# Windowed attention and a token expert layer: from eighty chunks in steps to forty units in a written order

## The chip, the cores and the metric

One core of a Trainium2 chip. The metric is device time in microseconds for one launch. The kernel before was run three times: 281.56, 281.57 and 285.97 us, median 281.57 us. The engines are named as the profile names them: PE (TensorE), with PEld for its weight loads, DVE (VectorE), ACT (ScalarE), POOL (GpSimd) and SP (SyncE, which issues most transfers).

## The reference

Eight batches, eight heads, 576 tokens, 64 numbers per head. Four heads see the 32 last keys, four see every fourth of the last 128 (again 32 keys). Then, for each batch, the 128 tokens with the highest gate score go through two dense layers:

```python
scores = scale * np.matmul(q, k.transpose(0, 1, 3, 2))
rel = pos[:, None] - pos[None, :]
mask_plain = (rel >= 0) & (rel < window)                                      # window 32
mask_dil = (rel >= 0) & (rel < window * dilation) & (rel % dilation == 0)     # dilation 4
scores = np.where(masks, scores, -1e9)
attn = softmax(scores)                       # maximum subtracted, sum + 1e-9
x = (attn @ v)                               # tokens x 512
...
scores = np.einsum('bsd,d->bs', x, w_gate)
for b in range(B):
    top_idx = np.argpartition(-scores[b], capacity)[:capacity]                # capacity 128
    xe = x[b, top_idx]
    ye = np.maximum(xe @ w1, 0.0) @ w2
    out[b, top_idx] = xe + g[:, None] * ye   # g = 1 / (1 + exp(-scores))
```

## The kernel before, in words

**Tiling.** A batch has ten chunks: four of the dilated heads with 128 queries each (one residue of the position modulo four), one with the last 16 queries of all residues, and five of the plain heads (four of 128 queries, one of 64). A group of 32 queries sees a window of 64 keys. `scores` (L165 to L194) lays a chunk's windows side by side in one PSUM bank of tag `s`, of which there are two; each product has 64 rows and 64 columns. Partitions are pairs of heads and queries.

**A chunk's way.** `maximum` (L219) adds the mask and takes the maximum of each window in one fused instruction of DVE, followed by a read of the accumulator. L224 subtracts the maxima, on POOL for nine chunks of ten once the first steps are past. `transposes` (L233 to L258) turns the differences on PE into a single bank `t` and ACT writes their exponentials. `attend` (L276, L281) multiplies by the values, each key with a column of ones so that the divisor comes along, into one of two banks `a`. `normalise` adds a small number to the divisor (L291), inverts it (L293) and divides, either on DVE in one instruction (L296) or on ACT in four (L301). SP stores the rows (L314).

**Choosing the tokens.** `route` sums each chunk's rows with the gate's weights on DVE (L356), brings the dilated scores into token order through DRAM (L367, L368), spreads all scores over the partitions with PE (L379), copies them to SBUF with ACT (L381), counts on DVE for each token how many are higher (L388), marks the 128 ranks (L396, mostly POOL), and finds and gathers the rows (L406 to L412). 

**The experts.** The weights are split into two float32r parts, a rounded one and the rest (L333, L335, L336), and each product is three matmuls (L473, L490, L503). Rows of batches 2 and 3, 4 and 5, 6 and 7 are worked on together, those of 0 and 1 alone. The results come from `tag="m"`, three banks.

**The order.** A loop over 84 and more steps issues the pieces of several chunks: in step g the scores of chunk g, the turning of chunk g - 2, the values of g - 3 and the division of g - 4. The dictionary `T` says in which steps loads, placings (copies of the queries into their places, L121) and the choice happen; `work` hands out the experts' pieces by a rate. In the first 20 steps `scores` also issues three products with no use of their own (L171) to keep PE busy. Every engine executes its instructions in the order in which this loop issues them.

Of the kernel before, what the change touches and what calls it, by code (L numbers as in the profile page):

```python
# [9 lines left out]
F32 = mybir.dt.float32  # L10
# [28 lines left out]
T = dict(  # L39
    spd=(0, 5),  # steps in which the vector engine subtracts the maxima  # L40
    lqx=(0, 0),  # delay of the first of the later loads of queries
    warm=9,  # products that bring the tensor engine to its full clock while the first loads run
    sp=(0, 1, 2, 3, 5, 6, 7, 8, 9),  # chunks whose maxima GpSimd subtracts
    mp=(0, 1, 2, 3, 4),  # token tiles that GpSimd marks
    ne=(0, 1, 2, 3, 4, 5, 7, 8, 9),  # chunks that the vector engine divides in the first nb steps
    nb=25,
    pl1=(7, 7, 8, 8),  # steps at which the next dilated queries are put into their places, by pair and half
    pl0=(13, 11, 13, 10),  # the same for the plain ones
    pe1=(1, 1, 1, 1),  # 1: the scalar engine does it, 0: the vector engine
    pe0=(1, 1, 1, 1),  # L50
    lq1=10,  # steps of the loads of queries
    lq0=14,
    nv=(0, 2, 3, 4, 7, 9),  # chunks that the vector engine divides; the scalar engine does the others
    rep=3,  # more products with the mask in the first rn steps, which bring the tensor engine to its full clock
    rn=20,
    ro=10,  # step of the dilated gate scores' way into the tokens' order
    g4=14,  # step of the leftover's gate scores
    b0=(14, 15, (15, 15, 15, 17, 16), (15, 16, 15, 17, 16), 18, 20),  # steps of the choice in the first batch: total, spread, ranks, marks, pick, first use
    last=(14, 16, (16, 16, 17, 16, 16), (17, 17, 17, 17, 17), 21, 24),  # the same in the last batch
    mid=(15, 16, (16, 17, 18, 19, 20), (17, 20, 18, 20, 20), 22, 26),  # and in the others  # L60
    raw=(12, 21, 5),  # first steps of the loads of the two weights, and the delay of their split
    rate=(0.9, 0.65, 0.95, 0.9, 1.0),  # pieces of the experts' work in half a step, by group
    single=(0, 1, 5, 7),  # batches after which a tile alone is worked on
    extra=0,  # pieces that come before the step's exponentials
    gd=5,  # delay of the gate scores
    gd0=5,
    iq=(3, 4),  # steps of the first loads of the second batch's queries
    ip=3,  # step at which the first plain queries are placed
)
# [3 lines left out]
def tile_window_attention_moe(ctx, tc, qt, kt, va, vb, w_gate, w1, w2, masks, mask_l, ident, slots, toks, outs, capacity):  # L73
# [5 lines left out]
    ps = ctx.enter_context(tc.tile_pool(name="ps", bufs=2, space=PSUM))  # L79
# [4 lines left out]
    id32 = cp.tile([P, P], F32, name="id32")  # L84
    id16 = cp.tile([P, P], BF16, name="id16")
    mk = cp.tile([P, 2 * GK], BF16, name="mk")
    mkl = cp.tile([P, 2 * LK], BF16, name="mkl")
    thr_sb = cp.tile([P, 2 * 512 + HB], F32, name="thr_sb")
# [3 lines left out]
    toks_sb = cp.tile([P, NTOK], F16, name="toks_sb")  # L92
    qs = [cp.tile([P, 2, S // G, 2, G], F32, name=f"qs{i}") for i in range(2)]
# [3 lines left out]
    dts = [[cp.tile([P, (G if i else 0) + 4 * GK], F32, name=f"dt{i}_{j}") for j in range(3)] for i in range(2)]  # L97
    mss = [[cp.tile([P, 4 * GK], F32, name=f"ms{i}_{j}") for j in range(3 - i)] for i in range(2)]
    pts = [[cp.tile([P, 4, P], F32, name=f"pt{i}_{j}") for j in range(2)] for i in range(2)]
# [4 lines left out]
    warm = cp.tile([P, 512], BF16, name="warm")  # L104
    raw = {}
# [3 lines left out]
    def clear(kind, eng):  # L109
        eng.memset(qs[kind][HB:P, :, :, 0, :], 0.0)  # L110
        eng.memset(qs[kind][0:HB, :, :, 1, :], 0.0)

    def load_q(b, kind, lo=0, hi=S):
        nc.sync.dma_start(out=qw[kind][:, :, lo:hi], in_=qt[b, kind].rearrange("d (p s) -> d p s", p=2)[:, :, lo:hi])

    def load_k(b, kind, lo=0, hi=S):
        nc.sync.dma_start(out=ks[kind][:, :, lo:hi], in_=kt[b, kind].rearrange("d (p s) -> d p s", p=2)[:, :, lo:hi])

    def place(kind, h, eng, p0=0, p1=2, lo=0, hi=S):
# [5 lines left out]
    nc.gpsimd.memset(thr_sb, TINY)  # L125
    nc.gpsimd.affine_select(out=thr_sb, in_=thr_sb, pattern=[[-1, 2 * 512 + HB]], compare_op=ALU.is_gt, fill=0.0,
                            base=512, channel_multiplier=1)
# [3 lines left out]
    for kind in (1, 0):  # L131
        for j in range(2):
            nc.gpsimd.memset(pts[kind][j], 0.0)
        for j in range(3 * kind):
            nc.gpsimd.memset(dts[kind][j][:, 0:G], NEG)
        if kind:
            clear(0, nc.gpsimd)
            for j in range(2):
                nc.gpsimd.memset(mss[1][j][:, GK + G:2 * GK], NEG)
        else:  # L140
            nc.gpsimd.memset(mss[0][2][:, 0:G], NEG)

    def load_v(b, kind):
# [52 lines left out]
    def maximum(b, c, st):  # L196
# [14 lines left out]
        for u in range(n):  # L211
# [3 lines left out]
            else:  # L215
                m = mk[:, 0 if kind else GK:][:, 0:GK]
                if windows(c)[u][0] == 0 and c <= 5:
                    lo, hi = (0, G) if kind else (G, GK)
# [524 lines left out]
```

## Time and profile before

| | |
|---|---|
| median of three runs | 281.57 us |
| profiled execution, first to last instruction | 280.1 us |
| busy PE, DVE, ACT, POOL | 251.1, 205.8, 154.8, 128.1 us |
| mean granted clock of PE, as a share of 2.4 GHz | 0.971 |
| moved by DMA | 53.75 MB, mean 192 GB/s |

The profiled execution's own time is known as its span, 280.1 us from the first to the last instruction; the median of the runs is 1.5 us longer. In rows of the trace, "busy" time counts an instruction from its start to its modelled end, so that overlapping instructions may each be longer than the distance between their starts. A row of a window gives, for each engine, busy time and number of instructions in that stretch.

### The profile page before, as it was taken

To read this page: it belongs to the slowest core of one execution; us is meant where nothing else is said; L and a number is where in the kernel's file an instruction comes from. 1 tells how busy PE (TensorE), PEld (TensorE's weight loads), DVE (VectorE), ACT (ScalarE), POOL (GpSimd) and SP (SyncE) were. 2 spreads that over 40 slices of the span, in tenths; PEclk is the share of its full clock that TensorE was granted. 3 is DMA by queue.
4 is the path that set the end of the run, shared out by engine and by line. 5 is a ranking of instruction groups with operands and counts; after the bars stand their busy time and mean duration, and the time that the engine had idled before them with its cause. 6 is when DMAs were issued, how large, how long until landed. Compare 5 with 4: busy or idle time off the path is not lost. (4 is left out here: it accounts for less than half of the span.)

```text
span 280.1 us, 9042 instructions
## 1 busy us (share of the span) xinstructions
PE 251.1 (90%) x3245; PEld 194.2 (69%) x3245; DVE 205.8 (73%) x1152; ACT 154.8 (55%) x437; POOL 128.1 (46%) x153
## 2 busy tenths in 40 slices
PE   7799984789996978799998899999999989989992
PEld 3577763566764756477776688886777879869981
DVE  3887989757999886977998898769657986815211
ACT  2558855636583585787777878657565454012100
POOL 8123338837489953572485346227643451021011
PEclk9999999759999899999999999999999999999998
DMA  6998399766769498449765973964463113020010
GB/s 186 372 380 230 94 293 362 254 218 194 271 184 326 130 323 307 136 117 363 254 207 133 408 239 101 320 255 136 125 220 144 63 46 95 0 77 37 0 40 37
DMA packets 29998, 53.75 MB, mean 192 GB/s; under 512 B 9089, under 2 KB 20097, under 8 KB 28929
## 3 DMA queue, kind: packets, MB, share of 16 engines
q1 hardware_dynamic: 28240, 48.85, 53.0%
q0 software_dynamic: 1280, 4.20, 4.6%
q8 instruction: 26, 0.43, 0.7%
q10 hardware_dynamic: 432, 0.12, 0.2%
q14 instruction: 20, 0.16, 0.2%
HBM read 41.60 MB, written 11.55 MB: 190 GB/s over the span
## 5 line engine op out<-in xcount | busy, mean ns | idle before, releaser
L224 POOL TENSOR_TENSOR dt<-ms,mx 128x256 f32<-128x256 f32 (+1 forms) x68 | 51.7, 760 | 95.0 <-DVE mx L219 71.4
L219 DVE CUSTOM_DVE_ANT_0 ms<-s,mk 128x64 f32<-128x64 f32 (+1 forms) x272 | 43.5, 215 | 13.0 <-PE s L191 8.9
L281 PE MATMUL a<-vs,pt 128*64 128x65 f32 x1088 | 50.7, 232 | 2.5 <-DVE x L296 1.3
L281 PEld LDWEIGHTS a<-vs,pt 128*64 128x64 f32 x1088 | 40.6, 141 | 17.2 <-issue 4.1
L191 PEld LDWEIGHTS s<-ks,qs 128*64 128x64 f32 x1088 | 39.1, 142 | 16.6 <-issue 10.1
L191 PE MATMUL s<-ks,qs 128*64 128x64 f32 (+1 forms) x1088 | 48.3, 231 | 2.4 <-DMA ks<-in_kt_dram 2.1
L258 ACT ACTIVATE pt<-t 64x128 f32<-64x128 f32 (+2 forms) x128 | 34.7, 271 | 24.7 <-PE t L253 21.3
L247 ACT ACTIVATE pt<-t 64x256 f32<-64x256 f32 (+1 forms) x80 | 28.5, 356 | 25.6 <-PE t L243 24.3
L121 ACT COPY qs<-qw 64x576 f32<-64x576 f32 (+3 forms) x59 | 38.6, 676 | 5.2 <-DMA qw<-in_qt_dram 4.5
L388 DVE SCALAR_TENSOR_TENSOR junk<-sb,sc,thr_sb 128x576 bf16<-128x576 f32 (+1 forms) x40 | 36.8, 920 | 5.5 <-ACT sb L381 5.1
L356 DVE CUSTOM_DVE_ANT_0 junk<-x,wg 128x256 bf16<-128x256 f32 (+1 forms) x72 | 40.6, 564 | 0.0
L396 POOL TENSOR_SCALAR oh<-slots_sb,rk 128x128 f16<-128x128 f32 (+1 forms) x35 | 28.1, 809 | 4.1 <-DVE junk L388 4.1
L490 PE MATMUL ph<-xh,w1h 128*128 128x256 f32 x96 | 29.1, 303 | 0.5 <-ACT xh L439 0.5
L503 PE MATMUL py<-w2h,hh 128*128 128x512 f32 x64 | 28.8, 449 | 0.0
L503 PE MATMUL py<-w2l,hh 128*128 128x512 f32 x64 | 25.8, 403 | 2.0 <-POOL w2l L336 2.0
L301 ACT ACTIVATE x<-a,rin 128x64 f32<-128x64 f32 x100 | 23.1, 314 | 7.9 <-DVE rin L293 5.0
L490 PE MATMUL ph<-xl,w1h 128*128 128x256 f32 x96 | 27.0, 281 | 0.2 <-DVE xl L440 0.2
L490 PE MATMUL ph<-xh,w1l 128*128 128x256 f32 x96 | 26.8, 279 | 0.0
L510 POOL DMA_INDIRECT out_dram<-y,ix x8 | 8.5, 1059 | 40.0 <-DVE y L508 26.4
L503 PE MATMUL py<-w2h,hl 128*128 128x512 f32 x64 | 25.4, 397 | 0.0
L219 DVE DVE_READ_ACCUMULATOR2_ANT mx<- 128x1 f32 x288 | 23.9, 83 | 0.3 <-issue 0.2
L296 DVE TENSOR_TENSOR x<-a,rin 128x256 f32<-128x256 f32 (+1 forms) x55 | 23.0, 418 | 0.3 <-DVE mx L219 0.2
(89 smaller groups left out, 407.1 us busy)
## 6 DMA issues: line engine op xcount, KB each, us to landing
vs<-in_va_dram SPq DMA_DIRECT2D x8, 1170.0 KB, 8.0
qw<-in_qt_dram SPq DMA_DIRECT2D x15, 576.0 KB, 7.0
ks<-in_kt_dram SPq DMA_DIRECT2D x15, 576.0 KB, 5.2
out_dram<-x SPq DMA_DIRECT2D x64, 128.0 KB, 4.6
vs<-in_va_dram SPq DMA_DIRECT2D x8, 520.0 KB, 5.4
raw<-in_w_dram SPq DMA_DIRECT2D x16, 256.0 KB, 3.3
vs<-in_vb_dram SPq DMA_DIRECT2D x8, 195.0 KB, 5.4
out_dram<-x SPq DMA_DIRECT2D x32, 16.0 KB, 3.2
```

The source lines that it names most:

```text
L121: eng(qs[kind][r, p0:p1, lo // G:hi // G, h, :], qw[kind][r, p0:p1, lo:hi].rearrange("d p (g q) -> d p g q", q=G))
L191: nc.tensor.matmul(st[GK * p:GK * (p + 1), u * GK + lo:u * GK + hi], q[:, p, qg].rearrange("d h q -> d (h q)"), k[:, p, k0 + lo:k0 + hi], ...
L219: nc.vector.tensor_tensor_reduce(out=ms[:, u * wk_ + lo:u * wk_ + hi], in0=s3[:, u, lo:hi], in1=m[:, lo:hi], scale=1.0, scalar=-3.0e38, op ...
L224: (nc.vector if T["spd"][0] <= b * NCH + c < T["spd"][1] or c not in T["sp"] else nc.gpsimd).tensor_tensor(out=out.rearrange("q (u k) -> q ...
L247: nc.scalar.activation(pt[r].rearrange("k a (i u q) -> k u i a q", i=2, u=2)[:, u, 0:n], tt[r, 0:n * P].rearrange("k (i a q) -> k i a q", ...
L258: nc.scalar.activation(pt[r, :, g * G:(g + 1) * G], tt[r, i * P:(i + 1) * P].rearrange("k (a q) -> k a q", a=4), AF.Exp, scale=SCALE)
L281: nc.tensor.matmul(av[r, head, :], pt[:, 2 * p + h, r], v[:, c if kind else 2 * (c - 5) + i, vc], start=True, stop=True)
L356: nc.vector.tensor_tensor_reduce(out=junk[:n], in0=xs.pop((b, c))[:n], in1=wg[:n, o:o + 256], scale=UP, scalar=0.0, op0=ALU.mult, op1=ALU. ...
L388: nc.vector.scalar_tensor_tensor(out=junk[:n], in0=st["sb"][:n], scalar=st["sc"][:n, t:t + 1], in1=thr_sb[:n, o:o + S], op0=ALU.subtract, ...
L396: (nc.vector if last or t not in T["mp"] else nc.gpsimd).tensor_scalar(out=st["oh", s][:n, t, :], in0=slots_sb[:n, s * P:(s + 1) * P], sca ...
L490: nc.tensor.matmul(out, w[:, i, f * P:(f + 1) * P], x[:, i, :], start=i == 0 and k == 0, stop=i == 3 and k == 2)
L503: nc.tensor.matmul(pys[j], x[:, i, j * P:(j + 1) * P], w[:, i, :], start=i == 0 and k == 0, stop=i == 7 and k == 2)
```

## The change

The work is cut into 40 units, five a batch: two of two dilated chunks each (`d`), one of all leftovers (`l`: the residues' last queries and the plain heads' last 64), two of two plain chunks each (`p`). Every function works on a whole unit:

- Scores: eight windows of 64 columns fill one bank `st`, which is the only one. It is cleared once, and windows that lack a half are covered by wide masks made at the start (`mkd`, `mkp`).
- Mask, maximum and difference: one addition of the mask (`M`), one `tensor_reduce` (`X`) and one subtraction (`U`, on POOL for 33 units, on DVE for 7) of 512 columns instead of an instruction per window.
- Exponentials (`E`): the same instructions cover both chunks, 256 or 512 columns each.
- Values (`V`) go into one pair of banks, of which there is one; the divisor (`D`) and the division (`N`) take both chunks at once, and the division is always on DVE. The leftover unit is stored by ten small transfers (`O`).
- Gate sums: 12 units multiply on POOL (`G`) and sum on DVE; 20 units use two fused sums on DVE as before. The leftover's sums are one for all 512 numbers, after a readback.
- Ranks (`R`) read the spread scores directly in PSUM (two banks); the copies on ACT go. The table for draws becomes bfloat16.
- The weights' rounding is on ACT for all sixteen pieces. Of the 40 marks eight are on DVE.
- The filler products of the first 20 steps go. The warm-up is 18 products of 256 columns instead of 9 of 512.
- Experts: batch 0 and batch 7 alone, 1 and 2, 3 and 4, 5 and 6 together. Their banks `m` are two instead of three.
- The loop and `T` go: every piece has a name, and a text of 1190 names says the order in which they are issued. It interleaves attention, choice and experts freely. A few places of it, ahead of the core of the diff:

```
S18 M18 R2.2 X18 U18g K2.0.1g K2.0.0g R2.4 K2.0.4g K2.0.2g V16 D16 q4.0.0 R2.3 N16 Y0.0.5 S19
T17 E17.3 E17.2 E17.0 E17.1 p4.1.0.1.0a M19 X19 U19g G15 Y0.0.6 Y0.0.7 T18 V17 D17 K2.0.3v O16.0
...
```

(`S19` scores of unit 19, `p` placing, `q`, `k`, `v` loads, `w` loads of weights, `h` and `l` their parts, `b`, `K`, `t` the choice, `F`, `r`, `s`, `z` the first layer, `Y` the second; a last letter names the engine.)

```diff
-LT = 2            # steps from a chunk's scores to their turning
...
+ORDER = """
...
-    ps = ctx.enter_context(tc.tile_pool(name="ps", bufs=2, space=PSUM))
+    ps = ctx.enter_context(tc.tile_pool(name="ps", bufs=1, space=PSUM))
...
+    st = ps.tile([P, 512], F32, tag="s", name="st")
...
+    def product(p, g, kind, c0, k0, n):
+        nc.tensor.matmul(st[GK * p:GK * (p + 1), c0:c0 + n], qs[kind][:, p, g].rearrange("d h q -> d (h q)"),
+                         ks[kind][:, p, k0:k0 + n], start=True, stop=True)
...
+    def mask(u):
+        what, b, d = kind_of(u)
+        ms = keep(f"ms_{u}", wk, [P, 512], F32, "ms", 2)
+        masks_ = [mkd] if what == "d" else [mkp[:, d:d + 8, :]] if what == "p" else [mkl, mkp[:, 1:3, :]]
+        for (s3, w0, n), m, (o3, _, _) in zip(parts(u, st), masks_, parts(u, ms)):
+            nc.vector.tensor_tensor(out=o3, in0=s3, in1=m, op=ALU.add)
+
+    def maximum(u):
+        mx = keep(f"mx_{u}", wk, [P, 8], F32, "mx", 3)
+        for o3, w0, n in parts(u, kept[f"ms_{u}"]):
+            nc.vector.tensor_reduce(out=mx[:, w0:w0 + n], in_=o3, axis=AX.X, op=ALU.max)
+
+    def subtract(u, eng):
...
+                eng.tensor_tensor(out=o3, in0=i3, in1=mx[:, w0:w0 + n].unsqueeze(2).to_broadcast(list(i3.shape)),
+                                  op=ALU.subtract)
...
+    def attend(u):
+        what, b, d = kind_of(u)
+        av = kept[f"a_{u}"] = keep(f"a_{u}", ps, [P, 2, 512], F32, "a", 1)[:, :, 0:VW].rearrange(
+            "q a (h d) -> q a h d", h=4)
...
+    def divide(u):
+        av, rin, na = kept[f"a_{u}"], kept[f"rin_{u}"], 1 if kind_of(u)[0] == "l" else 2
+        x = keep(f"x_{u}", wk, [P, 2, 4, D], F32, "x", 3)
+        nc.vector.tensor_tensor(out=x[:, 0:na], in0=av[:, 0:na, :, 0:D],
+                                in1=rin[:, 0:na].unsqueeze(3).to_broadcast([P, na, 4, D]), op=ALU.mult)
...
+    def gate_terms(u):
+        o = 256 if u % NU < 2 else 0
+        gm = keep(f"gm_{u}", wk, [P, 2, 256], F32, "gm", 1)
+        nc.gpsimd.tensor_tensor(out=gm, in0=kept[f"x_{u}"].rearrange("q a h d -> q a (h d)"),
+                                in1=wg[:, o:o + 256].unsqueeze(1).to_broadcast([P, 2, 256]), op=ALU.mult)
...
+    def gate_sums(u):
+        nc.vector.tensor_reduce(out=sums(u), in_=kept[f"gm_{u}"], axis=AX.X, op=ALU.add)
...
+    def spread(b):
+        pa = keep(f"pa_{b}", ps, [P, 1024], F32, "pa", 1)
+        for t in range(NTOK):
+            nc.tensor.transpose(pa[:, t * P:(t + 1) * P], scs[b % 2][:, t:t + 1].to_broadcast([P, P]), id32)
...
+        nc.vector.scalar_tensor_tensor(
+            out=junk[:n], in0=kept[f"pa_{b}"][:n, 0:S], scalar=scs[b % 2][:n, t:t + 1], in1=thr_sb[:n, o:o + S],
+            op0=ALU.subtract, op1=ALU.is_gt, accum_out=kept[f"rk_{b}"][:n, t:t + 1])
...
+    for name in (ORDER.split() if nt == 1 else default_order(nt, groups)):
+        pieces[name]()
```

## Rows read from the trace of the kernel before

**Rows 1.** The page, engine table: busy us, share of the span, instructions.

```profile
PE 251.1 (90%) x3245; PEld 194.2 (69%) x3245; DVE 205.8 (73%) x1152; ACT 154.8 (55%) x437; POOL 128.1 (46%) x153
```

**Rows 2.** Windows: busy us (instructions) by engine, PE clock, DMA share, GB/s.

```profile
0.00:7.90 7.90, 5.06 (x31) 2.24 (x31) 3.46 (x7) 2.62 (x4) 7.11 (x18) 1.00 0.69 211
7.90:222.50 214.60, 195.79 (x2848) 147.91 (x2848) 175.90 (x1063) 140.32 (x400) 109.64 (x125) 0.97 0.71 232
222.50:274.90 52.40, 50.24 (x369) 44.01 (x368) 25.73 (x86) 11.84 (x34) 10.37 (x11) 1.00 0.13 40
274.90:280.10 5.20, 0.00 (x0) 0.00 (x0) 0.72 (x1) 0.00 (x0) 0.97 (x1) 0.75 0.13 50
```

**Rows 3.** Timeline, PE and PEld: start us, us, engine, line, operation.

```profile
120.69 0.55 PEld L281 LDWEIGHTS a<-vs,pt 128*64 128x64 f32 x16 [0.36 <-ACT h L476]
...
121.77 0.20 PEld L253 LDWEIGHTS t<-id,dt 128*128 128x128 f32 x2
...
238.08 0.28 PE L490 MATMUL ph<-xh,w1h 128*128 128x256 f32 x1
...
238.20 0.28 PE L490 MATMUL ph<-xh,w1l 128*128 128x256 f32 x1
...
239.02 0.40 PE L503 MATMUL py<-w2l,hh 128*128 128x512 f32 x1
...
239.26 0.40 PE L503 MATMUL py<-w2h,hl 128*128 128x512 f32 x1
```

**Rows 4.** Groups by line and form, PE: busy us, mean ns, idle before.

```profile
L171 PE MATMUL s<-warm,id 128*128 128x256 bf16 x60 | 10.2, 279 | 0.0
```

**Rows 5.** Groups by line and form, DVE.

```profile
L356 DVE CUSTOM_DVE_ANT_0 junk<-x,wg 128x256 bf16<-128x256 f32 x64 | 37.4, 584 | 0.0
L388 DVE SCALAR_TENSOR_TENSOR junk<-sb,sc,thr_sb 128x576 bf16<-128x576 f32 x32 | 30.0, 938 | 5.4 <-ACT sb L381 5.1
...
L293 DVE RECIPROCAL rin<-den 128x4 f32<-128x4 f32 x64 | 11.4, 178 | 2.2
L291 DVE TENSOR_SCALAR den<-a 128x4 f32<-128x4 f32 x64 | 9.7, 151 | 3.0 <-PE a L281 2.0 <-PE s L177 0.6 <-PE t L253 0.4
...
L447 DVE CUSTOM_DVE_ANT_0 junk<-xe,wg 128x512 bf16<-128x512 f32 x8 | 6.8, 849 | 0.1
...
L440 DVE TENSOR_TENSOR xl<-px,xh 128x512 fp32r<-128x512 f32 x8 | 5.5, 692 | 10.2 <-ACT xh L439 10.0
```

**Rows 6.** Timeline, DVE and POOL, three places.

```profile
120.17 0.23 DVE L219 CUSTOM_DVE_ANT_0 ms<-s,mk 128x64 f32<-128x64 f32 x1
...
120.72 0.42 DVE L296 TENSOR_TENSOR x<-a,rin 128x256 f32<-128x256 f32 x1
...
16.65 0.61 POOL L224 TENSOR_TENSOR dt<-ms,mx 128x256 f32<-128x256 f32 x1 [8.66 <-DVE mx L219]
16.75 0.80 DVE L356 CUSTOM_DVE_ANT_0 junk<-x,wg 128x256 bf16<-128x256 f32 x1
...
126.75 0.41 DVE L356 CUSTOM_DVE_ANT_0 junk<-x,wg 128x256 bf16<-128x256 f32 x1
```

**Rows 7.** Groups by line and form, POOL and ACT.

```profile
L224 POOL TENSOR_TENSOR dt<-ms,mx 128x256 f32<-128x256 f32 x60 | 46.3, 771 | 92.5 <-DVE mx L219 69.2 <-DVE sc L372 13.7 <-PE s L191 5.2
...
L336 POOL TENSOR_TENSOR w1l<-raw,w1h 128x512 fp32r<-128x512 f32 x8 | 11.4, 1428 | 5.4 <-ACT w1h L335 3.2 <-DVE w1h L333 1.9 <-DVE ix L408 0.4
...
L301 ACT ACTIVATE x<-a,rin 128x64 f32<-128x64 f32 x100 | 23.1, 314 | 7.9 <-DVE rin L293 5.0 <-issue 2.6
```

**Rows 8.** Windows of 46 to 52 us, and PE's timeline there.

```profile
46.00:48.00 2.00, 0.22 (x3) 0.20 (x4) 1.97 (x11) 0.57 (x2) 1.72 (x2) 1.00 1.00 373
...
50.00:52.00 2.00, 2.00 (x30) 1.67 (x32) 0.71 (x5) 1.34 (x3) 1.82 (x2) 0.50 0.32 105
...
50.45 1.14 PE L281 MATMUL a<-vs,pt 128*64 128x65 f32 x16
51.37 1.03 PE L191 MATMUL s<-ks,qs 128*64 128x64 f32 x16
```

More of the change, by code (lines that the diff above doesn't have):

```diff
@@ L36 @@
 VW = 4 * (D + 1)
-LT = 2
[L39 to L69, printed above, removed]
+NU = 5
@@ new lines, in pick, with index, gather @@
+    def pick(b, s):
+        pi = keep(f"pi_{b}_{s}", ps, [P, 512], F32, "m", 2)
+        for t in range(NTOK):
+            nc.tensor.matmul(pi[:, 0:1], oh_sb[s][:, t, :], toks_sb[:, t:t + 1], start=t == 0, stop=t == NTOK - 1)
+    def index(b, s):
+        nc.vector.tensor_copy(keep(f"ix_{b}_{s}", wk, [P, 1], I32, "ix", 6), kept[f"pi_{b}_{s}"][:, 0:1])
+    def gather(b, s):
+        m = min(P, capacity - s * P)
+        xe = keep(f"xe_{b}_{s}", wk, [P, DM], F32, "xe", 4)
+        if m < P:
+            nc.vector.memset(xe, 0.0)
+        nc.gpsimd.indirect_dma_start(
+            out=xe[:m], out_offset=None, in_=outs[b][:, :],
+            in_offset=bass.IndirectOffsetOnAxis(ap=kept[f"ix_{b}_{s}"][:m, 0:1], axis=0))
@@ L543, in tile_window_attention_moe @@
-    for _ in range(T["warm"]):
-        nc.tensor.matmul(pw, warm[:, 0:P], warm, start=True, stop=True)
-    load_q(0, 1, P, S)
-    load_k(0, 1, SR, S)
-    nc.scalar.dma_start(out=mkl, in_=mask_l)
-    nc.vector.tensor_copy(id16, id32)
-    for h in range(2):
-        place(1, h, nc.scalar.copy if h else nc.vector.tensor_copy, lo=0, hi=P)
-    for h in range(2):
-        place(1, h, nc.scalar.copy if h else nc.vector.tensor_copy, lo=P)
-    load_v(0, 1)
-    load_q(0, 0)
-    load_k(0, 0)
-    if nt:
-        nc.sync.dma_start(out=wg, in_=w_gate)
@@ new lines, in outer, with result @@
+    def outer(e, j, i):
+        b, s = e[j]
+        if i == 0:
+            keep(f"py_{b}_{s}", ps, [P, 512], F32, "m", 2)
+        hh, hl = hidden(e)
+        for (x, w, k) in ((hh, w2h, 0), (hh, w2l, 1), (hl, w2h, 2)):
+            nc.tensor.matmul(kept[f"py_{b}_{s}"], x[:, i, j * P:(j + 1) * P], w[:, i, :],
+                             start=i == 0 and k == 0, stop=i == 7 and k == 2)
+    def result(b, s):
+        y = keep(f"y_{b}_{s}", wk, [P, DM], F32, "raw", 4)
+        nc.vector.scalar_tensor_tensor(out=y, in0=kept[f"py_{b}_{s}"], scalar=kept[f"g_{b}_{s}"][:, 3:4],
+                                       in1=kept[f"xe_{b}_{s}"], op0=ALU.mult, op1=ALU.add)
@@ new lines, in draws, with warm_up @@
+    def draws():
+        nc.gpsimd.memset(thr_sb, TINY)
+        nc.gpsimd.affine_select(out=thr_sb, in_=thr_sb, pattern=[[-1, 2 * 512 + HB]], compare_op=ALU.is_gt, fill=0.0,
+                                base=512, channel_multiplier=1)
+    def warm_up():
+        pw = ps.tile([P, 512], F32, tag="m", bufs=2, name="pw")
+        for _ in range(WARM):
+            nc.tensor.matmul(pw[:, 0:256], warm[:, 0:P], warm, start=True, stop=True)
+    copies = {"a": nc.scalar.copy, "v": nc.vector.tensor_copy, "g": nc.gpsimd.tensor_copy}
@@ new lines, in tile_window_attention_moe @@
+    for u in range(B * NU):
+        what = kind_of(u)[0]
+        for name, f in (("S", scores), ("M", mask), ("X", maximum), ("T", turn_scores), ("V", attend), ("D", divisors),
+                        ("N", divide)):
+            piece(f"{name}{u}", f, u)
+        for a, eng in engines.items():
+            piece(f"U{u}{a}", subtract, u, eng)
+        for i in range(2 if what == "p" else 4):
+            piece(f"E{u}.{i}", weights, u, i)
+        for i in range(10 if what == "l" else 1):
+            piece(f"O{u}.{i}", store, u, i)
+        if what != "l" and nt:
+            piece(f"G{u}", gate_terms, u)
+            piece(f"H{u}g", gate_sums, u)
+            piece(f"H{u}v", gate_alone, u)
@@ new lines, in tile_window_attention_moe @@
+    for i in range(16 if nt else 0):
+        piece(f"w{i}", load_weights, i)
+        for a, eng in copies.items():
+            piece(f"h{i}{a}", weight_high, i, eng)
+        for a, eng in engines.items():
+            piece(f"l{i}{a}", weight_low, i, eng)
+    groups, ready = [], []
+    for b in range(B if nt else 0):
+        for n, f in enumerate((readback, gate_last, put_out, put_back, total, spread)):
+            piece(f"b{b}.{n}", f, b)
+        for t in range(NTOK):
+            piece(f"R{b}.{t}", rank, b, t)
+        for s in range(nt):
+            for t in range(NTOK):
+                for a, eng in engines.items():
+                    piece(f"K{b}.{s}.{t}{a}", mark, b, s, t, eng)
+            for n, f in enumerate((pick, index, gather, turn_rows, result, scatter)):
+                piece(f"t{b}.{s}.{n}", f, b, s)
+            for i in range(3):
+                piece(f"g{b}.{s}.{i}", gate_row, b, s, i)
+            ready.append((b, s))
+        while ready and (len(ready) > 1 or b in SINGLE):
+            groups.append(ready[:2])
+            del ready[:2]
```

914 lines of the change are left out of this document (462 added, 452 removed).

## The prediction

> **What bounds the kernel now.** I read the page's engine table first: no engine is busy throughout, PE at 90% and DVE at 73% lead [rows 1]. "Busy" counts overlapping pipelines, so next I took the windows, cut at three events: the first mask on the vector engine (7.9 us), the last block of scores (222.5 us) and the last matmul (274.9 us) [rows 2]. They show three regimes. Up to 7.9 us the first loads run. From 7.9 to 222.5 us all attention is issued, and DVE is busy 175.9 of 214.6 us, 82%. From 222.5 to 274.9 us PE is almost never idle: this is mostly expert work that attention pushed behind itself. The last 5.2 us hold only the final result and its scatter.
>
> For PE's real load I read the timeline, since spacing, not duration, is what a pipelined matmul costs [rows 3]. Sixteen instructions of scores or of values take 0.55 us (the span of their weight loads), a transposition about 0.10 us, a product of the experts 0.23 us with 512 columns (two starts 0.24 apart) and 0.115 with 256 (0.12 apart). Every float32 product is two instructions. Over the program: 136 blocks of sixteen 75; the half-size last units 7; 152 turns 15; experts 192 and 48 wide products 55, 288 narrow ones 33; gathered rows, spreads and picks 12; 60 filler products 7; warm-up 4. Together about 208 us. Some 50 of it lie behind 222.5 and 5 ahead of 7.9, so the middle stretch holds about 153 us of PE work in 214.6 us: PE waits there for 62 us. DVE waits for 39. So the stretch is set by two engines waiting for each other, the fuller of which is DVE. PE's total alone would permit far less than 280.
>
> **What the change does, part by part.**
>
> *Masks and maxima.* Before, one fused instruction per window; four windows take 0.55 us (120.17 to 120.72) [rows 6], 1.10 for the two chunks of a new unit. After: one add of 512 columns from PSUM, like the 692 ns subtraction [rows 5], and one maximum over 512 columns. No row shows such a maximum. Bounds: 0.42, the 256-column row [rows 6], and 0.85, the fused 512-column sum [rows 5]; I take 0.69, the nearest in size. So 1.38 against 1.10 in 32 units, and about 1.0 against 1.05 (0.55 by spacing for the leftover, half a chunk, a difference) in 8: DVE **+9 us** (0 to +14).
>
> *Divisors.* 151 and 178 ns now serve two chunks [rows 5]: 40 pairs instead of 80, **-13**. *Division.* DVE takes all: 32 of 0.69 and 8 of 0.42 is 25.4 against 55 of 0.42, **+2**; ACT loses 100 pieces, 23 us [rows 7].
>
> *Gate sums.* Before 80 sums, mean 0.58 for a chunk [rows 5]. After, 12 units send the product to POOL and leave DVE one 512-column sum (0.69); 20 units keep two sums of 0.58; the leftover's eight grow to 0.85. 38 against 45: **-7**. *Ranks* read PSUM instead of a copy; before 0.94 and not less than 0.69 x 576/512 = 0.78. At 0.85, 40 of them are **-3** (-6 to 0), and 6 us of copies leave ACT. *Weight roundings* move to ACT: eight of about 0.69, **-5.5**. Seven differences and eight marks come to DVE instead of a few: **+2**. DVE's sum: 205.8 - 15.5 = about 190.
>
> Why sums vary: the same 256-column gate sum took 0.41 us alone and 0.80 beside a POOL difference that started 0.10 earlier [rows 6]. The Trainium skill ("SBUF — State Buffer", section "Who interferes with whom") says that a vector instruction with two SBUF inputs contends with a GpSimd instruction that reads SBUF, and one with a single SBUF input does not. Ranks, masks and divisions would then be free of it, and by it the ranks would come at the lower bound, 0.78, 3 us less in all; the trace agrees for the gate sums.
>
> *POOL.* 33 differences and 12 gate products of 512 columns. Bounds: 0.77, a 256-column one, and 1.43, the weight remainder of 512 [rows 7]; I take 1.43, which has the size. 64 us, marks 27 (32 of about 0.86, estimated from half-size differences), remainders 25, indirect transfers 17, placings and memsets 20: about 153, from 128. In units 4 to 17 the written order gives it 13 differences, 4 products, all 16 remainders, 9 marks, 3 placings, 2 transfers: 62 us, beside 59 on DVE. So POOL nearly ties there, and hides only if little goes wrong.
>
> *PE.* The same products; the 60 fillers go (10.2 us busy [rows 4], 7 by spacing). About 201. *DMA* moves the same data; its share of 0.71 in the stretch [rows 2] becomes 0.71 x 214.6/187 = 0.81. The ten small stores of a leftover unit stand in SP's queue, between loads; a load behind a store that waits comes late, a cost I put at zero since loads are issued a unit or more ahead, and at a unit (4.5 us) each if not.
>
> *Buffers.* Scores have one PSUM bank instead of two, the values' result one pair instead of two, the experts' bank two instead of three. So the next scores wait for the mask that reads the last ones, and the next values for the division: 0.69 and latency, and 0.33 + 0.69 and latency. In the order other PE pieces stand between. I walked units 18 to 22 with the prices above: five scores start at 0, 2.9, 7.8, 10.8 and 14.2 us, and PE is idle about 1.0 us in 14.2.
>
> *The end.* The last group holds one batch instead of two, and less waits for the last tokens. Behind the last scores the order leaves PE 32 pieces of three 512-column products (22.1), 96 narrow and 24 wide products (16.5), two blocks of values, and turns, picks and spreads (6): 45 us. Its own turn of hidden rows must wait for a copy, a subtraction and semaphores, about 3 us.
>
> **The sum.** DVE before the first mask stays near 4.5 and behind the last scores near 26 (before: 25.7 + 0.7 [rows 2]), so the stretch keeps 190 - 30.5 = 160 us. Its length is 160/u. Before, u was 0.82. The walked units give above 0.9, the start with POOL level and loads near their limit less; I take 0.86: 186 us, in which PE's 151 us are 81% (before 71%). End: 7.9 + 186 + 45 + 3 + 5.2 = 247 of span; with unrounded terms 248.3. The profiled execution spans 280.1 against a median of 281.57, 1.5 more, which I keep: **250 us** (u from 0.80 to 0.92: 264 to 238).
>
> **The rivals.**
>
> *The clock falls.* PE stood 46 to 48 us nearly idle (0.22 busy) at a granted clock of 1.00; at 50 to 52 it had 0.50, that is 1.2 instead of 2.4 GHz, and two blocks of sixteen started 0.92 apart instead of about 0.55 [rows 8]. The fillers held such gaps shut in the first 20 chunks. Without them PE has some 32 us of work in units 0 to 13, beside 41 on DVE. At the low level that is 32 x 0.92/0.55 = 54 us; with 0.95 us of waits a unit (38 in 40 units, below) and 5 us ahead it is 72, against 7.9 + 41/0.86 = 56: about 16 us more, **266 us**. For it: thin PE work early. Against it: in the windows as a whole the clock stayed at 0.97 [rows 2]. The Trainium skill ("TensorE: Matmul & The Clock Gate", section "A second HAM failure mode: psum-queue depth-cycling") tells of a kernel whose short idles between groups made the clock go back and forth; it speaks against this change. By that rule the time is this rival's.
>
> *The waits only move.* Larger pieces and single buffers keep PE waiting as long as before, 62 us or somewhat more. Then 5 + 151 + 62 = 218 for the last scores, and 218 + 53.2 + 1.5 = 273; up to 14 us more waiting is no change, **280**. For it: DVE's load falls by only 15 us, POOL's grows by 25. Against it: the walked units.
>
> *Turns (slower).* PE and DVE take turns at the single buffers. Place: scores behind the mask, values behind the division. Price for a unit: 0.69 + 0.25 and 0.33 + 0.69 + 0.30, 2.26 us, 90 over 40 units. If all of it shows, the last scores come at 5 + 151 + 90 = 246 and the time is **301 us**. It decides from the point where 287.2 is passed: 287.2 - 1.5 - 53.2 - 156 = 76.5 of the 90 exposed. For it: one bank each. Against: my forecast exposes 38, and the order has other pieces there.
>
> **How the numbers follow.** Chances: forecast 0.60 with its range 238 to 264; tighter, 234 to 238, 0.05; clock 0.11; waits move, 275 to 287, 0.12; turns beyond 287, 0.12. A range of 234 to 279 leaves out turns and most of the waits, 0.2. A change within 2% (276 to 287 us) can't be told from none. Faster 0.76, same 0.12, slower 0.12.
>
> **What would show it.** Right: windows with DVE near 86% until the last scores at about 194 us; masks and maxima near 0.69 each; POOL near 150 us busy; 45 us of dense PE behind the last scores. Wrong: a clock of 0.50 over several early windows; scores waiting for the vector engine's mask by a microsecond or more in most units; maxima over 0.85; POOL 512-column pieces over 1.75; or vector instructions waiting for POOL's products.

## The result, and the profile after

| | before | after |
|---|---|---|
| median | 282.71 us (4 runs, three of them those above) | 262.82 us (4 runs, 259.4 to 267.14) |
| ratio, 95% interval | | 0.9224 (0.916 to 0.9288) |
| profiled execution, span | 281.57, 280.1 us | 264.4, 262.7 us |
| forecast | | 250 us, own range 238 to 264, wide range 234 to 279 |

The ratio leaves out executions that the chip disturbed (of the four of the changed kernel it keeps 261.25 and 259.4 us), so it stands below the quotient of the medians, 0.930. The gain is 20 us by the medians and 22 by the ratio. The change is faster, as forecast, and the time lies in the range, but near its upper end: by the median it is 13 us longer than the number, by the ratio 10. Those 10 to 13 us are what the runs below look for. Where kernels are compared, the difference of their ratios, times 282 us, stands beside that of their medians.

The page of the changed kernel: busy time of each engine; the granted clock of PE and the busy share of the DMA engines in 40 slices; the chain that ended last.

```profile
PE 223.5 (85%) x3194; PEld 191.8 (73%) x3194; DVE 193.0 (73%) x520; ACT 105.7 (40%) x228; POOL 125.6 (48%) x154
...
PEclk9999986689999999799999999999999999999999
DMA  6997899888977799989644899886593154111001
...
PE 41%; DMA 30%; DVE 11%; issue 7%; SPq 5%; POOL 3%; ACT 2%; POOLq 0%; DVEq 0%; ACTq 0%
```

DVE has 193.0 us of work against 205.8 [rows 1], in 520 instructions instead of 1152. DMA has 30% of the chain. The page of the kernel before follows its chain for only 18% of the span and gives no comparison; a variant of it with other groups of experts, run below, has 9%.

The windows of after, cut at the same three events as before (columns as in [rows 2]):

```profile
0.00:8.47 8.47, 6.00 (x50) 4.37 (x50) 4.18 (x12) 2.12 (x3) 3.78 (x10) 1.00 0.73 228
8.47:208.80 200.33, 170.25 (x2793) 147.38 (x2795) 163.92 (x438) 95.75 (x210) 109.86 (x131) 0.96 0.80 244
208.80:257.40 48.60, 47.27 (x358) 40.02 (x353) 24.14 (x71) 7.86 (x16) 11.03 (x13) 1.00 0.21 66
257.40:262.70 5.30, 0.01 (x1) 0.00 (x0) 0.75 (x1) 0.00 (x0) 0.97 (x1) 0.98 0.13 49
```

The cut at 208.80 is the start of the last block of scores, as before; the runs below are cut at the start of that block's last product, 0.9 us later. Against [rows 2] the middle stretch fell from 214.6 to 200.3 us and what lies behind it from 57.6 to 53.9. In the stretch DVE is busy 163.92 of 200.33 us, 0.82: the same utilisation as before, where I had forecast 0.86. That is the open question: DVE has less to do, but waits as large a share of the time.

Pieces of the chain that ended last, in order of time (start, us, what), say on what:

```profile
30.21 6.23 DMA vs<-in_va_dram
36.57 1.50 PE a L399 x32
40.13 8.91 DMA ks<-in_kt_dram
49.17 1.98 PE st L269 x32
...
93.82 11.00 DMA ks<-in_kt_dram
104.95 1.57 PE st L269 x29
...
118.76 9.08 DMA ks<-in_kt_dram
127.97 1.15 PE st L269 x28
```

Four times this chain runs through a load of keys or values, 6 to 11 us from issue to landing. The scores of unit 9 start at 33.4 us, those of unit 10 at 49.2, behind the load issued at 40.13 (an expectation below calls them units 7 and 8; by the written order they are 9 and 10). PE was not idle all that time, since values and turns stand between. What ended its idle time (us in total, times, longest):

```profile
PE a L399 <- DVE x L412: 5.4, 5, 2.4
PE st L269 <- DMA ks<-in_kt_dram: 3.7, 5, 1.3
PE a L384 <- DMA vs<-in_vb_dram: 2.9, 2, 1.7
...
PE st L269 <- DVE ms L309: 2.4, 3, 0.9
...
PE a L399 <- DMA vs<-in_va_dram: 2.0, 1, 2.0
```

Loads ended 8.9 us of PE's idle time, with a smaller row of 0.3. If they cost more than that, it is by way of the other engines and buffers.

### The profile page after: what moved, and what is told of

It reads as the page before. It is cut to its first block, busy times and chain, and to the rows that moved or that the text cites. A ratio compares the mean times of both kernels' runs of the same rounds, so it can differ in the third digit from the quotient of the medians.

```text
span 262.7 us, 7956 instructions
## 1 busy us (share of the span) xinstructions
PE 223.5 (85%) x3194; PEld 191.8 (73%) x3194; DVE 193.0 (73%) x520; ACT 105.7 (40%) x228; POOL 125.6 (48%) x154
## 2 busy tenths in 40 slices
DMA packets 31284, 54.22 MB, mean 206 GB/s; under 512 B 9360, under 2 KB 20880, under 8 KB 30224
## 4 chain that ended last, share of the span: by engine, by line
PE 41%; DMA 30%; DVE 11%; issue 7%; SPq 5%; POOL 3%; ACT 2%; POOLq 0%; DVEq 0%; ACTq 0%
DMA ks<-in_kt_dram 13%; PE py L638 11%; PE ph L585 8%; PE a L399 7%; PE st L269 6%; DMA out_dram<-x 6%; DMA vs<-in_va_dram 5%; DMA xd<-out_dram 4%; DVE x L412 2%; DMA raw<-in_w_dram 2%; POOL w2l L453 2%; ACT ptd L368 2%; PE t L339 1%; SPq L429 1%; DVE ms L309 1%
## 5 line engine op out<-in xcount | busy, mean ns | idle before, releaser
L269 PE MATMUL st<-ks,qs 128*64 128x64 f32 (+1 forms) x1088 | 43.6, 234 | 6.7 <-DMA ks<-in_kt_dram 3.7
L269 PEld LDWEIGHTS st<-ks,qs 128*64 128x64 f32 x1088 | 38.9, 148 | 11.4 <-issue 4.9
L242 ACT COPY qs<-qw 64x576 f32<-64x576 f32 (+1 forms) x46 | 29.6, 655 | 20.2 <-DMA qw<-in_qt_dram 9.8
L368 ACT ACTIVATE ptd<-t 64x256 f32<-64x256 f32 (+2 forms) x64 | 23.6, 377 | 31.6 <-PE t L339 22.9
L399 PE MATMUL a<-vs,ptd 128*64 128x65 f32 x512 | 21.6, 238 | 11.9 <-DVE x L412 5.0
L516 DVE SCALAR_TENSOR_TENSOR junk<-pa,sc,thr_sb 128x576 bf16<-128x576 f32 (+1 forms) x40 | 30.8, 804 | 0.1
L328 POOL TENSOR_TENSOR dt<-ms,mx 128x512 f32<-128x512 f32 (+2 forms) x30 | 21.4, 727 | 19.2 <-DVE mx L314 13.7
L412 DVE TENSOR_TENSOR x<-a,rin 128x512 f32<-128x512 f32 (+1 forms) x40 | 25.4, 636 | 5.4 <-DMA out_dram<-x 2.4
L314 DVE TENSOR_REDUCE mx<-ms 128x8 f32<-128x512 f32 (+2 forms) x48 | 26.1, 558 | 0.7
L399 PE MATMUL a<-vs,ptp 128*64 128x65 f32 x512 | 20.0, 235 | 1.9 <-ACT ptp L368 0.8
```

Of the source, the lines that this page charges most:

```text
L242: eng(qs[kind][r, p0:p1, lo // G:hi // G, h, :], qw[kind][r, p0:p1, lo:hi].rearrange("d p (g q) -> d p g q", q=G))
L269: nc.tensor.matmul(st[GK * p:GK * (p + 1), c0:c0 + n], qs[kind][:, p, g].rearrange("d h q -> d (h q)"), ks[kind][:, p, k0:k0 + n], start=T ...
L314: nc.vector.tensor_reduce(out=mx[:, w0:w0 + n], in_=o3, axis=AX.X, op=ALU.max)
L328: eng.tensor_tensor(out=o3, in0=i3, in1=mx[:, w0:w0 + n].unsqueeze(2).to_broadcast(list(i3.shape)), op=ALU.subtract)
L368: nc.scalar.activation(out, src, AF.Exp, scale=SCALE)
L399: nc.tensor.matmul(av[i * HB:(i + 1) * HB, a, 2 * h + p], pt, values(1 if what == "d" else 0, j, 2 * h + p), start=True, stop=True)
```

## The experiments

The leading theory: loads of keys, values and queries, which I had priced at zero, land late and hold PE, and through it DVE. The rivals: the clock falls without the fillers; the chain through the single PSUM banks sets the pace; DVE's work does. Two more questions are why loads come late (bytes, or place in SP's queue), and where the 20 us that were gained come from.

### The changed kernel again

> The changed kernel again, unchanged, as the anchor of this set and for a second profile: 258 to 263 us (ratio to the kernel before 0.915 to 0.93). Every theory gives the same here; what it decides is where the granted clock falls. If the clock is at 1.00 all through this profile and the time is still about 260, the fall to 0.6 around 40 to 59 us in the first profile belonged to that execution and not to the kernel.

263.05 us median (257.68 to 266.32), ratio 0.9192 (0.9066 to 0.9319). Its profile has the clock low at other places than the first:

```profile
PEclk9999986988959977999999999979999999999998
```

The first had its dips in slices 6 to 9 and 17; this one is low in several places between slices 6 and 16, and once in slice 27. Around slices 6 to 10 the clock is low in both; where else it falls differs from one execution to the next.

### Without the later loads

```diff
-    v0.1.1 ... k1.1.0 ... q1.0.0 ... k1.0.0 ... v1.1.0 ...
+    (all q, k, v loads of batches 1 to 7 struck out of the written order)
```

> All loads of queries, keys and values behind batch 0's are left out, and their copies into the block layout work on batch 0's data again (the output is that of batch 0's inputs). Theory 1 (late loads are what keeps VectorE at 0.82 of the stretch): 160 to 164 us of work at 0.88 to 0.9 gives a stretch of 180 to 186, so 238 to 247 us. Rival 3 (the chain scores, mask, turn, weights, values over single PSUM buffers sets the pace): 256 to 261 us, for no load stands in that chain. Between these: both have a share, by where it falls.

245.53 us median (243.43 to 247.01), ratio 0.868 (0.8593 to 0.8766). The stretch, in its windows:

```profile
6.86:192.00 185.14, 166.59 (x2825) 144.83 (x2825) 166.12 (x442) 96.29 (x211) 109.03 (x134) 0.96 0.35 105
```

Same PE, DVE, ACT and POOL work, and 185.1 us instead of 200.3: utilisation 0.90. Loads are worth 15 us by the ratios (0.9224 - 0.868) and 17 by the medians. The clock of the stretch is 0.96 in both, so the difference is not the clock's. Rival 3 is left with little: the chain over single banks allows 185 us.

### The same loads, thin

```diff
     def load_k(b, kind, lo, hi):
+        hi = hi if b == 0 else lo + G
         nc.sync.dma_start(out=ks[kind][:, :, lo:hi], ...)
     # load_q alike; load_v: one tile instead of four or nine where b > 0
```

> Every load of queries, keys and values behind batch 0's keeps its place, its waits and its semaphores, but carries only a first slice (32 of 576 columns, one value tile of four or nine); the rest of each buffer keeps batch 0's data, so the output is not the reference's. The run without these loads stood at 245.5 us. If it is the bytes (each load takes long to land, and the DMA engines are near their limit): 244 to 249 us, as without the loads. If it is the place in SyncE's queue and the single buffers (a load is issued late): 255 to 261 us, as with full loads.

247.18 us median (245.62 to 247.64), ratio 0.882 (0.8748 to 0.8891): 15.6 us less than the changed kernel by the medians, 11 by the ratios, which is most of what leaving the loads out gave. Place in the queue, buffers, waits and number of issues are those of the changed kernel; only bytes are gone (28.37 MB moved instead of 54.22).

```profile
7.56:190.80 183.24, 165.74 (x2824) 143.85 (x2825) 164.11 (x442) 95.97 (x210) 109.30 (x133) 0.97 0.45 128
```

The same DVE work as after, 164.1 us, now takes 183.2 us, utilisation 0.896. So these 11 to 16 us are a matter of bytes on the way. DMA issues (columns: what, count, KB each, median us to landing), first of after, then of this run:

```profile
vs<-in_va_dram SPq DMA_DIRECT2D x8, 1170.0 KB, 9.2
qw<-in_qt_dram SPq DMA_DIRECT2D x15, 576.0 KB, 5.8
ks<-in_kt_dram SPq DMA_DIRECT2D x15, 576.0 KB, 7.0
out_dram<-x SPq DMA_DIRECT2D x32, 256.0 KB, 5.1
...
raw<-in_w_dram SPq DMA_DIRECT2D x16, 256.0 KB, 6.4
```

```profile
out_dram<-x SPq DMA_DIRECT2D x32, 256.0 KB, 2.3
raw<-in_w_dram SPq DMA_DIRECT2D x16, 256.0 KB, 4.3
...
ks<-in_kt_dram SPq DMA_DIRECT2D x14, 32.0 KB, 3.5
```

Stores and weight loads were not touched, yet land in 2.3 instead of 5.1 us and 4.3 instead of 6.4. Thin loads thus shorten every transfer beside them. How much of the time comes from the loads' own landing and how much from the others' (the stores free the result's buffers, the read-backs feed the ranks) this run does not separate. PE's idle time that a load ended falls only from 8.9 to 3.3 us, which points to a large part of the others.

### Thin loads in the kernel before

The same edit in the kernel before.

> The kernel before, with the same thin loads behind batch 0's (32 of 576 columns, one value tile; the output is not the reference's). If the loads' bytes were as dear to the kernel before as to the changed one (15 us): 264 to 269 us, and the gain of the change is not from them. If the kernel before was held by its engines and the loads were hidden: 278 to 284, and the loads became a bound only by the change.

277.34 us median (276.26 to 277.45), ratio 0.9865 (0.9787 to 0.9943).

```profile
7.38:218.80 211.42, 195.85 (x2852) 147.62 (x2854) 176.48 (x1063) 140.40 (x399) 110.35 (x126) 0.97 0.39 113
```

The bytes cost the kernel before 3.7 us (1.6 to 6 by the interval of its ratio), and the changed one 11 to 16. Neither expected band is met (it lies just under the second), but the second theory is the nearer: the kernel before mostly hid its loads, and the change uncovered them. Transfers were slowed in the kernel before as well: its own stores, 128 KB each, land in 4.6 us with all bytes and in 2.1 with thin loads. What differs is what the slowness cost. Without the bytes the change would have taken the time from 277.3 to 247.2, 30 us. With them 20 to 22 us are left.

### Small stores on ScalarE's queue

```diff
-            nc.sync.dma_start(out=dst, in_=x[q0:q0 + 16, 0, 0:2]...)
+            nc.scalar.dma_start(out=dst, in_=x[q0:q0 + 16, 0, 0:2]...)
     # and the two stores of its plain half
```

> The ten small stores of each leftover unit are issued from ScalarE's queue instead of SyncE's, so that loads no longer stand behind them. Theory 1, part a (loads come late because they stand behind waiting stores): 244 to 255 us, and the gap of 15.8 us between the scores of units 7 and 8 shrinks below 8. Theory 1, part b (loads come late because the DMA engines are busy at 0.8 or because each single buffer comes free late): 257 to 263 us. Rival 2 (clock) and rival 3 (the turns' and scores' single banks): 257 to 263. If ScalarE is the worse place because it then waits for each division: 263 to 270.

306.8 us median (304.83 to 308.6), ratio 1.0871 (1.0763 to 1.0979): much worse, beyond every expectation. ACT's timeline at the first leftover unit:

```profile
24.73 2.74 ACTq L429 DMA_DIRECT2D out_dram<-x  x4
27.52 0.59 ACT L368 ACTIVATE ptp<-t 64x512 f32<-64x512 f32 x1 [4.24 <-DMA out_dram<-x]
27.57 0.37 ACTq L429 DMA_DIRECT2D out_dram<-x  x1
28.12 0.59 ACT L368 ACTIVATE ptp<-t 64x512 f32<-64x512 f32 x1
29.04 1.17 ACTq L432 DMA_DIRECT2D out_dram<-x  x2
```

The stores' issues, and before them their wait, stand in ACT's own order between exponentials, each 0.4 to 0.7 us, and the values wait for those. On an engine that computes, a store that waits was dearer here than on SP. The mean granted clock was 0.873 here, so how much of the 44 us is the issues' own time stays open. The Trainium skill ("DMA: Bandwidth & Descriptors", section "Rules for kernel authors") says that spreading transfers over issuing engines gives no bandwidth and only saves issue time. Of bandwidth this run shows nothing; it adds that the issue time comes out of the new engine. So this run does not tell what SP's queue costs; the thin loads did.

### Loads moved ahead

Most loads of keys and values were moved in the written order to right behind the last reader of their buffer.

> Order only: each load of keys and values is moved in the written order to right behind the last reader of its buffer, ahead of the 1 to 24 stores and weight loads that stood between. If lateness comes from the place in the queue: 247 to 254 us, and the 15.8 us gap around 33 to 49 us shrinks below 9. If it comes from the bytes in flight: 257 to 263. If stores that are now later hold the three x buffers, VectorE waits for those: 262 to 270.

286.67 us median (283.79 to 288.09), ratio 1.0164 (1.0043 to 1.0285). Outside all bands. SP's timeline, first of after, then of this run, shows one fault of the edit:

```profile
10.40 0.43 SPq L252 DMA_DIRECT2D vs<-in_va_dram  x1
16.54 0.33 SPq L238 DMA_DIRECT2D ks<-in_kt_dram  x1
```

```profile
18.41 0.33 SPq L247 DMA_DIRECT2D vs<-in_va_dram  x1
...
21.69 0.43 SPq L251 DMA_DIRECT2D vs<-in_va_dram  x1
```

L251 here is L252 of after, batch 0's plain values. It was issued 11.3 us later, since the next batch's values (L247), which have to wait for unit 1 to be done with theirs, now stood ahead of it. So this is no clean test of the theory. It shows that in SP's queue, worked in order, a load issued as early as its buffer allows may be worse than one issued when due. Where the rest of the 24 us went I have not followed.

### Values in slices

```diff
-            nc.sync.dma_start(out=v, in_=va[b, :, 4 * VW:13 * VW]...)
+            for j, n in ((8, 1), (0, 4), (4, 4)):
+                nc.sync.dma_start(out=v[:, j:j + n], in_=va[b, :, (4 + j) * VW:(4 + j + n) * VW]...)
     # and the dilated half's four tiles two by two
```

> The changed kernel with the same bytes and the same order, but each load of values cut by the unit that reads it: two loads of two tiles for the dilated half, and one, four and four tiles for the plain half, so that the first reader waits only for its own slice. If what hurts is the landing time of the slice that is read next: 252 to 258 us. If it is the sum of the bytes in flight (keys and queries stand behind them anyway), or the three more issues a batch in SyncE's queue: 259 to 265 us.

262.39 us median (260.97 to 263.64, 6 runs), ratio 0.9296 (0.9233 to 0.9359): no gain. Its stretch is 199.13 us at a DMA share of 0.80, as after's. A finer grain of the same bytes does not help. Either it is the sum on the way and not the last slice of one load of values, to which the thin loads point, or the three more issues a batch take back what the slices gave; this run does not tell them apart. Keys in slices were not tried.

### Fillers put back

Seventeen groups of three filler products, 51 in all (the expectation below counts 51 groups), ahead of the scores of the first ten units and the values of the first seven.

> The changed kernel with 51 groups of three filler products (the mask product of before, into a bank not otherwise used then) placed ahead of the scores and values of the first half, as the kernel before had them. Theory 1 (loads come late): the clock in 40 to 60 us may rise from 0.73, but the time stays within 258 to 264 us, since the engine waits there for keys and values anyway. Rival 2 (the clock falls because the fillers are gone): the stretches of 0.73 and 0.91 to 0.93 cost 20 x 0.27 + 40 x 0.08 = about 8 us, so 250 to 254 us.

262.73 us median (259.87 to 265.71), ratio 0.9279 (0.914 to 0.9418): no change. Two of its windows of 20 us:

```profile
20.00:40.00 20.00, 16.69 (x340) 13.63 (x341) 13.86 (x38) 11.04 (x24) 10.73 (x13) 0.99 0.79 234
40.00:60.00 20.00, 17.62 (x297) 14.68 (x297) 16.46 (x43) 12.94 (x27) 13.90 (x16) 0.75 0.93 305
```

The fillers by their line (ns shortest, median and longest; us of the first and the last start):

```profile
L679 PE MATMUL pf<-warm x51: 272/273/421, 4.9 to 35.5; 128*128 128x256 bf16 x51
```

The last filler starts at 35.5 us, so none stands from 40 us on, where the clock is low. From 20 to 40 us it is 0.99 (after: 0.93). Behind the fillers it falls all the same: 0.75 of 2.4 GHz from 40 to 60 us, a mean over stretches at 2.4 and at 1.2, where after had 0.73 and the kernel before, whose last fillers start at 48.8 us, 0.81. So the run says that these early fillers save no time; whether fillers in the low windows would is not tested. That the missing time is not the clock's rests on the runs without loads and with thin ones: 0.96 and 0.97 in their stretches, 0.96 in after's.

The run shows one thing more: among PE's waits, listed down to 0.3 us, none is for a load here, and the time is the same as after's. So PE waiting for a load is not the only way in which the bytes cost time. In this run's chain the stores of results stand first among the transfers, with 9.1% of the span.

### Mask and maximum fused, with full and with thin loads

```diff
-            nc.vector.tensor_tensor(out=o3, in0=s3, in1=m, op=ALU.add)
-    (one tensor_reduce a unit for the maxima)
+            for w in range(n):
+                nc.vector.tensor_tensor_reduce(out=o3[:, w], in0=s3[:, w], in1=m[:, w], ...,
+                                               op0=ALU.add, op1=ALU.max, accum_out=mx[:, w0 + w:w0 + w + 1])
```

> One part undone: mask and maximum as in the kernel before, one fused instruction a 64-column window (8 a unit) instead of one mask and one maximum. By the prices of both traces 8 x 0.14 = 1.10 us against 1.37 a unit, so VectorE has 40 x 0.27 = 11 us less to do. If VectorE's work sets the pace: 248 to 253. If the waits for loads do, what it does less it waits more: 257 to 262. If the scores' bank is held 0.41 us longer a unit and that sets the pace: 266 to 276.

262.49 us median (260.02 to 267.11), ratio 0.9331 (0.9241 to 0.9421).

```profile
7.36:212.00 204.64, 176.29 (x2823) 151.95 (x2825) 157.64 (x908) 96.59 (x211) 111.48 (x134) 0.91 0.77 241
```

DVE has 6 us less to do in the stretch (157.6 against 163.9; I had expected 11) and the stretch is no shorter. So less work on DVE alone does not bring less time while the loads have all their bytes; as the fused form also holds the scores' bank longer, this run does not say whether DVE's work would count by itself.

> The changed kernel with thin loads (247.2 us) and mask and maximum fused a window, as before the change. VectorE has 6 us less to do (157.6 against 163.9 us in the stretch by the run with full loads, which was no faster for it). If VectorE's work sets the pace once the loads' bytes are gone: 239 to 243 us. If something else does (the single scores' bank, which the fused form holds longer): 246 to 252.

251.03 us median (249.18 to 252.27), ratio 0.8947 (0.8859 to 0.9036), where thin loads alone gave 247.18 (245.62 to 247.64). Here less work on DVE comes with 4 us more, or 1.6% (the executions of the two do not overlap, the intervals of their ratios just do). What PE waited for, first with thin loads and separate instructions, then fused:

```profile
PE st L273 <- DVE ms L313: 1.5, 2, 0.9
```

```profile
PE st L273 <- DVE mx L315: 5.5, 6, 1.5
```

The next scores wait for the last reader of the single bank. Separate, that is the mask (0.69 us), and the maximum works on SBUF beside the next scores; fused, the whole 1.10 us (two chunks by [rows 6]) hold the bank. The 4 us more of this wait fit the 4 us of time, though other waits moved too (for the division 3.8 to 0.7 us, for the queries' placing 0.2 to 2.5). So "one mask a unit" costs DVE time and gives PE its bank back sooner, and by these two runs the second is worth more. The prediction booked only the first.

### The written order, and the last group

> The changed units in the order that the kernel's rule gives when there is no written one (the fallback in the same file). If the written order is where the gain over the kernel before comes from: 272 us or more. If the units and the shorter list of instructions are: 258 to 266.

369.79 us median (367.12 to 371.5), ratio 1.319 (1.3054 to 1.3327). With the rule that the file falls back on, the same units take 107 us more than with the written order. That rule also gives POOL other work (all the gate products among it; POOL is 20% of this run's chain), and it is not the order of the kernel before, so the 107 us are no measure of what the written order gained over that. How the gain divides between larger pieces and the order stays open.

```diff
-    single=(0, 1, 5, 7),
+    single=(0, 7),
```

> The kernel before with the change's groups alone: batches 0 and 7 by themselves, the rest in pairs. The stretch behind the last scores was 57.6 us before and 53.0 to 53.9 after. If the single last group gives this 4 us: 276 to 279 us. If the planner of the kernel before puts other work there instead: 280 to 285.

282.24 us median (280.95 to 284.65), ratio 1.0057 (1.0019 to 1.0095). Its last two windows (the second up to the end):

```profile
7.84:213.00 205.16, 184.15 (x2812) 141.24 (x2812) 173.87 (x1045) 136.37 (x394) 106.87 (x123) 0.97 0.74 241
213.00:281.00 68.00, 60.30 (x410) 52.10 (x405) 30.74 (x102) 15.26 (x41) 12.57 (x14) 1.00 0.13 40
```

With the change's groups the kernel before finishes its scores 10 us sooner and works 10 us longer behind them: the planner only moves expert work. The grouping gains nothing by itself.

## Why the prediction was right, and where not

**Sign and mechanism.** Two ways of reading the four stretches give the gain. With all bytes: DVE work 175.9 to 163.9 us at 0.82 both times. With thin loads: 211.4 to 183.2 us, of which 12.4 us less work is 12.4/0.835 = 15 us (0.835 is 176.48/211.42) and a rise of the utilisation to 0.896 the other 13. This is bookkeeping that fits what the prediction said of larger units, and its walked units, "above 0.9", were near: 0.896 once the bytes are gone. It is not shown that DVE's work sets the time (6 us less of it in the fused run saved nothing), nor what the larger units gain apart from the written order. Unnamed time in the chain ("issue") fell from 20.3% of the span in the kernel before with thin loads to 7.1% in the changed one, 56 to 17 us.

**The step that failed** is the term for loads: "a cost I put at zero since loads are issued a unit or more ahead", and with it the rise of u from 0.82 to 0.86. The zero was meant for a load that stands behind a waiting store. The thin loads keep that place in the queue and lose the cost, so what the sum lacked is a term for the bytes. The share of the DMA engines was forecast at 0.81 and measured at 0.80, so the bytes were right; I did not ask what such a share does to the time to landing. Thin loads take 15.6 us off the median, 11 by the ratios, and u is 0.82 with the bytes and 0.896 without. The likely reading is that the work became shorter over the same bytes, so that what was hidden came out. The change also altered the places of the loads in the order, and no run changed only the one of the two. My u of 0.86 was meant to hold a little of this ("loads near their limit") and held too little. In numbers, 250 to the profiled 264.4: DVE's stretch work 163.9 instead of 160 is 3.9/0.86 = 4.5 us, u 0.818 instead of 0.86 is 163.9 x (1/0.818 - 1/0.86) = 9.8, start and end 0.6 + 0.7, and my rounding upward in the sum gives 1.2 back. The list of what would show it wrong had no row for loads at all.

**The prices.** Vector engine, groups by line and form:

```profile
L516 DVE SCALAR_TENSOR_TENSOR junk<-pa,sc,thr_sb 128x576 bf16<-128x576 f32 x32 | 25.1, 806 | 0.1
L412 DVE TENSOR_TENSOR x<-a,rin 128x512 f32<-128x512 f32 x32 | 22.1, 689 | 5.0 <-DMA out_dram<-x 2.4 <-DMA srd<-sr 1.4 <-DMA qw<-in_qt_dram 0.2
L314 DVE TENSOR_REDUCE mx<-ms 128x8 f32<-128x512 f32 x32 | 21.8, 682 | 0.7
L478 DVE CUSTOM_DVE_ANT_0 junk<-x,wg 128x256 bf16<-128x256 f32 x40 | 17.4, 477 | 0.1
...
L309 DVE TENSOR_TENSOR ms<-st,mkp 128x512 f32<-128x512 f32 x16 | 11.0, 685 | 2.0 <-PE st L269 1.7 <-POOL dtd L321 0.3
```

Mask and maximum are 0.69 and 0.68, forecast 1.38 together; the division 0.689, forecast 0.69; ranks 0.806 against 0.938 [rows 5], forecast 0.85; the gate sums that stay whole 0.477 against 0.584 [rows 5], forecast unchanged. Together 193.0 against a forecast of 190, in part by luck: ranks (31.5 us) and gate sums (32.4) came out 8 us below the 34 (40 of 0.85) and 38 of the sum, and other terms above, such as differences and marks on DVE with 8.6 us, where I had added 2 to the 2.9 of the kernel before. GpSimd:

```profile
L522 POOL TENSOR_SCALAR oh<-slots_sb,rk 128x128 f16<-128x128 f32 x26 | 16.2, 624 | 12.5 <-DVE junk L516 9.4 <-DMA slots_sb<-in_slots_dram 2.9
L460 POOL TENSOR_TENSOR gm<-x,wg 128x512 f32<-128x512 f32 x12 | 15.4, 1280 | 9.5 <-DVE x L412 8.5 <-DVE sw L470 0.9
L328 POOL TENSOR_TENSOR dt<-ms,mx 128x512 f32<-128x512 f32 x14 | 14.6, 1042 | 9.3 <-DVE den L406 4.0 <-DVE mx L314 3.9 <-DVE ix L531 1.3
```

The 512-column difference takes 1.04 us; of my two bounds, 0.77 and 1.43, I took the upper, and marks take 0.62, not 0.86. POOL's 153 us were 125.6. POOL has 3% of after's chain, so this is not likely to have saved time.

**The end.** 48.6 + 5.3 = 53.9 us behind the last scores, forecast 45 + 3 + 5.2 = 53.2. This step was right.

**The signs.** Of the signs of being right, masks and maxima near 0.69 came true and 45 us behind the last scores nearly; DVE near 86%, last scores at 194 us (208.8) and POOL near 150 us did not.

**The rivals.** *Clock:* its sign showed, 0.50 from 40 to 44 and from 48 to 52 us in after, and the median is nearer to its 266 us than to my 250. But the stretch keeps a mean of 0.96 with all loads and without them, and 0.97 with thin ones; a step of 0.01 over 200 us is about 2 us. So the missing time is not the clock's, and I take the nearness for chance. The kernel before also fell to 0.50 at 50 us [rows 8], just behind its fillers, so these did not hold every gap shut. The Trainium skill ("TensorE: Matmul & The Clock Gate", section "A second HAM failure mode: psum-queue depth-cycling") tells of a kernel whose short idles between groups made the clock go back and forth, at a cost in throughput; the trace agrees that the clock goes up and down, not that this rival's time is lost to it. *Waits only move:* half right. They did move, from engine to DMA, and took back 8 to 11 of 30 us. *Turns:* in after scores waited 2.4 us in all for the mask and values 5.4 for the division, 7.8 of the 76.5 us that this rival needed. Held longer, the bank goes with 4 us more in the fused run.

No run here beats the changed kernel clearly while doing the same work. What the runs point to, fewer bytes (the plain values are loaded twice, in overlapping tiles), was not tried.

## What to carry to other kernels

When a change shortens the compute over the same bytes, work out the new DMA share and give the loads a price: at a share of 0.71 they cost 4 us here, at 0.80 they cost 11 to 16. To price loads apart from their place in a queue, make them thin: keep each issue, wait and buffer, and carry a slice. And a buffer that one engine frees and another waits for is best read last by the shortest instruction, even if that makes the reader's total work larger; here that was worth about 4 us, once the loads' bytes were gone.

## What the runs showed of the hardware that I had not expected

- Transfers that nobody touched landed in half the time (256 KB stores 5.1 to 2.3 us) when the loads beside them lost their bytes; in the kernel before, 128 KB stores 4.6 to 2.1 us.
- A 512-column float32 difference took POOL 1.04 us, a product of the same size 1.28, the weight remainder that writes float32r 1.33 to 1.37: the columns alone do not give the price.
- With the ten small stores of each leftover unit on ScalarE's queue the time rose by 44 us over eight batches (262.8 to 306.8), at a mean granted clock of 0.873.
